# Query and key projections by Strassen's scheme, gate steps with one operand in PSUM, and a new order

## The chip, the cores and the metric

One core of a Trainium2 chip runs one program. The metric is the device time of one execution in microseconds, as the median of several runs. The engines are named as in the profile: PE is TensorE's matmul, PEld its weight load, DVE is VectorE, ACT is ScalarE, POOL is GpSimd, SP is SyncE, whose queue issues every transfer here.

## The reference

Two sequences of 768 tokens with 512 features pass through three layers, all in 32-bit floats.

```python
# 1 retention, 8 heads of 64, per token t
state = gamma * state + outer(k[t], v[t]);  x[t] = q[t] @ state / 8
# 2 channel MLP (2048 wide)
x = x + relu(norm(x) * g @ w1) @ w2
# 3 mixture of 4 attention experts (width 64), no residual
logits = x @ w_gate                     # the two best experts of each token, softmax over them
for e in range(4):
    q, k, v = x @ wq[e], x @ wk[e], x @ wv[e]
    a = softmax(causal(q @ k.T / 8))
    out += gate[:, e] * (a @ v @ wo[e])
```

## The kernel before

Tokens are handled in six chunks of 128 per sequence `b` and, in the wide layers, in two blocks `j` of 384 (`TB`). Each operand of a wide product is kept as a rounded high half and a rest (`h`, `l`; `x` holds `XH` and `XL`), and a product is three matmuls: high by high, high by rest, rest by high.

The stages are these.

- **Retention**, `r_tile`: for each of the twelve tiles (b, chunk) scores, `intra`, `inter`, a state update and two transposes on PE, with masks, norm and splitting on DVE, ACT and POOL. Its inputs `kq` and `vk` and the first weight pieces `raw` come in over SP.
- **Channel MLP**: eight slices `f` of 256 hidden features. For f = 0 and 1 `m_h` makes the hidden block and `m_c` multiplies it by the second weights and adds to the running sum `xT`. For f = 2 to 7 (`SEVEN`) the hidden block of a sequence is made by `m_h7`, which uses Strassen's scheme: seven products (six matmuls each) where eight would be needed, over a two by two split of weights (by `S`, made in `w_sums` on POOL) and of tokens and features (by `t`, made once per sequence in `x_sums` on POOL and ACT). The partial results are combined with `keep` (ACT copies PSUM to `u`) and `add` (DVE). The last slice ends with new `XH`, `XL` for the third layer.
- **Projections**: `q_proj` makes queries and keys of one block (two halves of the contraction, six matmuls each), `q_val` makes values and logits of a chunk, `gates` turns the logits of a block into weights with twelve small DVE instructions and one on ACT.
- **Attention**: `a_scores` (PE, DVE, ACT, DVE, POOL in turn), `a_turn` (transposes), `a_value`, `a_out`, sequence 0 first, with the work of sequence 1 between.

All instructions are steps of a planner, `Plan`. A step names an engine, a cost, what it reads and writes and its buffers; its priority is its place in the program plus a bias plus a number of the table `RANK`, and `issue` lets each engine take the ready step with the lowest priority whose buffers have room. What comes out is a fixed order on each engine, and buffers at fixed places (`PL`). The same table decides when each transfer is issued. PSUM has eight banks, `ps`. At the start PE fills time with matmuls on a constant tile (`spin`).

## Time and profile before

| | |
|---|---|
| median of 3 runs | 439.39 us (438.41 to 439.47) |
| the profiled execution's own time | 436.77 us |
| its span in the trace | 435.0 us |
| PE busy | 426.4 us, 98% of the span |
| PEld, DVE, ACT, POOL busy | 401.7, 300.6, 216.3, 213.5 us |
| clock granted to PE | full in every slice |

The profiled execution took 1.8 us more than the span of its trace, and 2.6 us less than the median of the runs. A busy PE counts matmuls of any tile, the constant ones of the start too.

### The profile page before, as it was taken

The numbers are of one execution on the slowest core, as the hardware profiler recorded it, in microseconds if no ns is written. First come the engines' busy times: TensorE is split into PE (matmuls) and PEld (weight loads), VectorE is DVE, ScalarE is ACT, GpSimd is POOL, SyncE is SP. The second block draws the span as 40 slices with busy tenths as digits, with TensorE's granted clock in tenths as the row PEclk, the third lists the DMA queues.
The fourth block names the chain that finished last, engine by engine and source line by source line (L and its number), as shares of the span: only waits on it lengthen the run. The fifth ranks groups of instructions, "written<-read, shape, count | busy, mean of one in ns | idle before, by whom it ended". The sixth has DMA issues, their size and how long they took to land.

```text
span 435.0 us, 9093 instructions
## 1 busy us (share of the span) xinstructions
PE 426.4 (98%) x3546; PEld 401.7 (92%) x3546; DVE 300.6 (69%) x756; ACT 216.3 (50%) x458; POOL 213.5 (49%) x224
## 2 busy tenths in 40 slices
PE   8998999999999999999999999999999999999996
PEld 7777998999999999999999999999999899877875
DVE  2769999855558876966966764458936776778762
ACT  1568676242557436436336234324621775778540
POOL 1777877999999616416316126400130533251530
PEclk9999999999999999999999999999999999999999
DMA  7999723200232202303304001102000000010212
GB/s 270 327 343 319 232 83 111 105 2 0 87 108 98 98 2 96 99 0 100 95 2 132 15 1 35 63 2 75 23 6 2 2 2 0 3 50 26 75 60 88
DMA packets 11995, 35.18 MB, mean 81 GB/s; under 512 B 1840, under 2 KB 2480, under 8 KB 11952
## 3 DMA queue, kind: packets, MB, share of 16 engines
q1 hardware_dynamic: 11952, 34.60, 23.2%
q8 instruction: 28, 0.46, 0.4%
q14 instruction: 15, 0.12, 0.1%
HBM read 31.45 MB, written 3.15 MB: 80 GB/s over the span
## 4 chain that ended last, share of the span: by engine, by line
PE 91%; DVE 2%; DMA 1%; issue 0%; POOL 0%; ACT 0%; SPq 0%; POOLq 0%
PE ps L791 31%; PE ps L861 20%; PE ps L769 8%; PE ps L955 8%; PE ps L1124 4%; PE ps L979 4%; PE ps L425 4%; PE ps L1050 4%; PE ps L1151 4%; PE ps L613 1%; DMA vk<-in_vk_dram 1%; PE ps L584 1%; PE ps L621 1%; PE ps L603 0%; DVE xT L633 0%; DVE ps L695 0%
## 5 line engine op out<-in xcount | busy, mean ns | idle before, releaser
L791 PE MATMUL ps<-h,w 128*128 128x384 f32 x768 | 144.3, 335 | 0.0
L791 PEld LDWEIGHTS ps<-h,w 128*128 128x128 f32 x768 | 133.8, 188 | 0.7 <-issue 0.2
L797 DVE TENSOR_TENSOR xT<-xT,ps 128x384 f32<-128x384 f32 x112 | 60.6, 551 | 32.6 <-PE ps L791 31.9
L1080 POOL TENSOR_SCALAR pr<-pr,sm,gate 128x384 f32<-128x384 f32 (+5 forms) x48 | 33.9, 718 | 66.4 <-ACT pr L1065 26.0
L722 POOL TENSOR_TENSOR w<-wy,w 128x512 fp32r<-128x512 f32 x26 | 33.4, 1296 | 42.1 <-PE ps L791 39.7
L861 PE MATMUL ps<-t,S 128*128 128x384 f32 x216 | 42.2, 335 | 0.0
L861 PEld LDWEIGHTS ps<-t,S 128*128 128x128 f32 x216 | 37.7, 188 | 0.3 <-DVE wy L698 0.3
L769 PE MATMUL ps<-x,w 128*128 128x384 f32 x192 | 35.4, 337 | 0.0
L688 ACT ACTIVATE wx<-raw 128x512 f32<-128x512 f32 x32 | 21.7, 678 | 26.2 <-DVE ps L695 15.4
L1065 ACT ACTIVATE pr<-pr,sm 128x384 f32<-128x384 f32 (+5 forms) x48 | 31.7, 662 | 5.2 <-DVE sm L1057 5.1
L769 PEld LDWEIGHTS ps<-x,w 128*128 128x128 f32 x192 | 33.2, 188 | 0.5 <-DVE xT L797 0.2
L870 ACT ACTIVATE u<-ps 128x384 f32<-128x384 f32 x36 | 17.4, 489 | 31.5 <-PE ps L861 24.9
L880 ACT ACTIVATE h<-ps 128x384 fp32r<-128x384 f32 x48 | 23.1, 488 | 18.6 <-PE ps L791 13.2
L875 DVE TENSOR_TENSOR ps<-ps,u 128x384 f32<-128x384 f32 x36 | 20.3, 563 | 16.4 <-ACT u L870 10.3
L690 POOL TENSOR_SCALAR wx<-wx 128x512 f32<-128x512 f32 x32 | 19.8, 618 | 23.2 <-ACT wx L688 22.7
L861 PE MATMUL ps<-x,w 128*128 128x384 f32 x144 | 28.5, 334 | 0.0
L882 DVE SCALAR_TENSOR_TENSOR h<-ps,h 128x384 fp32r<-128x384 f32 x48 | 26.0, 551 | 2.8 <-ACT h L880 2.7
L692 DVE TENSOR_SCALAR ps<-wx 128x512 uint32<-128x512 uint32 x32 | 22.0, 688 | 4.9 <-POOL wx L690 4.9
L861 PEld LDWEIGHTS ps<-x,w 128*128 128x128 f32 x144 | 25.3, 188 | 0.0
L720 ACT ACTIVATE w<-wy 128x512 fp32r<-128x512 f32 x26 | 16.3, 628 | 17.2 <-PE ps L791 17.0
L698 DVE SCALAR_TENSOR_TENSOR wy<-raw,ps 128x512 uint32<-128x512 uint32 x32 | 21.9, 684 | 3.8 <-POOL sf L738 2.1
L1057 DVE CUSTOM_DVE_ANT_0 pr<-ps,mask 128x384 f32<-128x384 f32 (+4 forms) x48 | 22.0, 495 | 2.3 <-PE ps L1050 2.1
(116 smaller groups left out, 797.7 us busy)
## 6 DMA issues: line engine op xcount, KB each, us to landing
raw<-in_w_dram SPq DMA_DIRECT2D x32, 512.0 KB, 3.5
kq<-in_kq_dram SPq DMA_DIRECT2D x11, 512.0 KB, 5.5
vk<-in_vk_dram SPq DMA_DIRECT2D x9, 512.0 KB, 5.6
out_dram<-ob SPq DMA_DIRECT2D x11, 256.0 KB, 2.0
vk<-in_vk_dram SPq DMA_DIRECT2D x4, 256.0 KB, 5.3
vraw<-in_wv_dram SPq DMA_DIRECT2D x1, 520.0 KB, 3.4
kq<-in_kq_dram SPq DMA_DIRECT2D x2, 256.0 KB, 2.9
mraw<-in_wk_dram SPq DMA_DIRECT2D x1, 512.0 KB, 3.6
```

Of the source, the lines that this page charges most:

```text
L692: DVE(0.69, lambda: dve.tensor_scalar(u32(z), u32(x), 4, 1, op0=OP.logical_shift_left, op1=OP.logical_shift_right), r=[x], w=[z])
L722: POOL(1.3, lambda: pool.tensor_tensor(f32r(l), f32(y), f32(h), OP.subtract), r=[y, h], w=[l])
L769: pe.matmul(f32(pa, TB), lhsT=wt, rhs=blk(f32r(xt[b][j]))[:, k], start=(n == 0), stop=(n == 11))
L791: pe.matmul(f32(pa, TB), lhsT=wt, rhs=t, start=(n == 0), stop=(n == 5))
L797: DVE(0.55, lambda: dve.tensor_tensor(blk(f32(xt))[:, k], blk(f32(xt))[:, k], f32(pa, TB), OP.add), r=[pa] + [(xt, cc, w) for cc in range( ...
L861: pe.matmul(f32(pa, TB), lhsT=wt, rhs=t, start=(first and n == 0), stop=(n == 5), skip_group_check=True)
L880: ACT(0.49, lambda: act.activation(f32r(h, TB), f32(src, TB), AF.Relu), r=[src], w=[h])
L882: DVE(0.55, lambda: dve.scalar_tensor_tensor(f32r(l, TB), f32(src, TB), 0.0, f32(h, TB), op0=OP.max, op1=OP.subtract), r=[src, h], w=[l])
L955: pe.matmul(f32(pa, TB), lhsT=mw(n, lo, k, p * 128, (p + 1) * 128), rhs=blk(f32r(xt))[:, k], start=(i == 0), stop=(i == 11))
L1057: DVE(0.22 + wide * 1.04e-3, lambda ks=ks, n=n, z=z, SC=SC: dve.tensor_tensor_reduce(f32(PR[z])[:, ks], f32(SC[z])[:, :wide], f32(MASK)[:, ...
L1065: ACT(act_c(nk) + .18, lambda pr=pr, z=z: act.activation(f32(pr, nk), f32(pr, nk), AF.Exp, bias=f32(sm)[:, z:z + 1], scale=-1.0, accum_out ...
L1080: POOL(0.34 + nk * 0.84e-3, lambda pr=pr, z=z, e=e: pool.tensor_scalar(f32(pr, nk), f32(pr, nk), f32(sm)[:, 6 + z:7 + z], GT[b, j][:, cc, ...
```

## The change

- `q_proj` is now one call for a sequence and a weight: seven products of six matmuls over a two by two split, where four blocks of twelve matmuls stood. It brings `keep` and `add` steps, and buffers `uq`.
- The split weights `Sq` of `wk` and `wq` are made in `load_mw` on POOL (four small operations, one large) and ACT.
- The split tokens `t` have to be made anew from the third layer's input: `x_sums(b, False)` runs for both sequences at the end of the channel MLP, four subtractions and four rests on POOL and four copies on ACT each. For that the last `m_c` also writes its result to `xT` on ACT.
- In `gates` one operand of each two-operand step lies in PSUM, behind one more copy; each of its two DVE steps takes a PSUM bank.
- In `q_phase` the values and gates come ahead of queries and keys, queries and keys of the two sequences change places in memory, and `pr` has eleven buffers where it had twelve.
- All numbers of `RANK` are new, so the order on every engine is.

```diff
-    "q_proj 1": (32, (137, -8, -29, -4, 36, 0, 0, -70)),
...
-    "x_sums 2": (8, (-50, -134, 8, -63, 8, 11, -28, -102)),
...
+    "q_proj 1": (28, (8, -5, -10, -14, 50, -3, 112, 73)),
...
+    "x_sums 2": (16, (1, 0, -66, 56, -9, 0, -18, 20)),
...
+    PL["Sq"] = region(o_z, 4 * KB, 2) + region(o_h + 28 * KB, 4 * KB, 2)
+    PL["uq"] = region(o_z + 8 * KB, 3 * KB // 2, 4)
...
-    PL["qk0"] = region(o_r, 3 * KB, 8)
-    PL["vv0"] = region(o_r + 36 * KB, KB, 6)
+    PL["qk0"] = region(o_h, 3 * KB, 8)
+    PL["vv0"] = region(o_h + 36 * KB, KB, 6)
...
-    PL["qk1"] = region(o_h, 3 * KB, 8)
-    PL["vv1"] = region(o_h + 36 * KB, KB, 6)
-    PL["pr"] = region(o_xt, 3 * KB, 8) + region(o_h + 24 * KB, 3 * KB, 4)
+    PL["qk1"] = region(o_r, 3 * KB, 8)
+    PL["vv1"] = region(o_xt + 18 * KB, KB, 6)
+    PL["pr"] = region(o_xt, 3 * KB, 6) + region(o_r + 36 * KB, 3 * KB, 4) + region(o_h + 24 * KB, 3 * KB, 1)
...
         ACT(0.49, lambda: act.activation(blk(f32r(xh))[:, k], f32(pa, TB), AF.Copy),
...
         P.at = "m_c 5"
+        ACT(0.49, lambda: act.activation(blk(f32(xt))[:, k], f32(pa, TB), AF.Copy), r=[pa], w=[(xt, "k", k)])
+        P.at = "m_c 6"
         DVE(0.55, lambda: dve.tensor_tensor(blk(f32r(xl))[:, k], f32(pa, TB), blk(f32(xh))[:, k], OP.subtract),
-            r=[pa, (xh, "k", k)], w=[(xl, "k", k)] + (keys(xl) if k == 0 else []))
+            r=[pa, (xt, "k", k), (xh, "k", k)], w=[(xl, "k", k)] + (keys(xl) if k == 0 else []))
 
...
-    def x_sums(b):
+    def x_sums(b, own=True):
         th, tl = TH[b], TL[b]
         both = lambda fn, r, w: POOL(1.85, lambda: fn(pool), r, w)
-        for t, kh, j in ((2, 0, 1), (0, 0, 0), (1, 1, 1), (3, 1, 0)):
+        for t, kh, j in ((2, 0, 1), (0, 0, 0), (1, 1, 1), (3, 1, 0)) if own else ():
             cs = slice(kh * TW, (kh + 1) * TW)
             P.at = "x_sums 1"
             both(lambda en, t=t, j=j, cs=cs: en.tensor_tensor(plain(tl[t]), f32(XH[b][j])[:, cs], f32(XL[b][j])[:, cs], OP.add),
                  keys(XH[b][j]) + keys(XL[b][j]), [tl[t]])
-        for t, p, q in ((0, 2, 0), (2, 1, 2), (1, 1, 0), (3, 3, 1)):
+        xs = {2: (0, 1), 0: (0, 0), 1: (1, 1), 3: (1, 0)}
+
+        def part(t, new):
+            if own or new:
+                return lambda: plain(tl[t]), [tl[t]]
+            kh, j = xs[t]
+            return lambda: f32(XT[b][j])[:, kh * TW:(kh + 1) * TW], [(XT[b][j], "k", 2 * kh + k) for k in range(2)]
+
+        for t, p, q, made in ((0, 2, 0, ()), (2, 1, 2, ()), (1, 1, 0, (0,)), (3, 3, 1, (1,))):
+            (xp, rp), (xq, rq) = part(p, p in made), part(q, q in made)
             P.at = "x_sums 2"
-            both(lambda en, t=t, p=p, q=q: en.tensor_tensor(plain(tl[t]), plain(tl[p]), plain(tl[q]), OP.subtract),
-                 [tl[p], tl[q]], [tl[t]])
+            both(lambda en, t=t, xp=xp, xq=xq: en.tensor_tensor(plain(tl[t]), xp(), xq(), OP.subtract), rp + rq, [tl[t]])
         for t in range(4):
             P.at = "x_sums 3"
             ACT(0.84, lambda t=t: act.activation(f32r(th[t]), plain(tl[t]), AF.Copy), r=[tl[t]], w=[th[t]])
...
         P.at = "load_mw 3"
         POOL(2.4, lambda: pool.tensor_tensor(f32r(l, sz), f32(raw, sz), f32(h, sz), OP.subtract), r=[raw, h], w=[l])
...
+        if n in ("wk", "wq"):
+            sh, sl = new("Sq"), new("Sq")
+            at = lambda i, m: f32(raw)[:, 512 * i:512 * i + 512].rearrange("p (k m c) -> p k m c", k=2, m=2)[:, :, m]
+            part = lambda i: plain(sl)[:, 256 * i:256 * i + 256].rearrange("p (k c) -> p k c", k=2)
+            for i, p, q, op in ((0, lambda: at(0, 1), lambda: at(1, 1), OP.add),
+                                (1, lambda: part(0), lambda: at(0, 0), OP.subtract),
+                                (2, lambda: at(0, 0), lambda: at(0, 1), OP.subtract),
+                                (3, lambda: at(1, 0), lambda: part(1), OP.subtract)):
+                P.at = "load_mw 4"
+                POOL(0.76, lambda i=i, p=p, q=q, op=op: pool.tensor_tensor(part(i), p(), q(), op), r=[raw], w=[sl])
+            P.at = "load_mw 5"
+            ACT(1.1, lambda: act.activation(f32r(sh), plain(sl), AF.Copy), r=[sl], w=[sh])
+            P.at = "load_mw 6"
+            POOL(2.41, lambda: pool.tensor_tensor(f32r(sl), plain(sl), f32(sh), OP.subtract), r=[sl, sh], w=[sl])
+            MW[n, "S"] = (sh, sl)
...
-    def q_proj(b, j, n, p):
-        cs = slice(j * TB, (j + 1) * TB)
-        pa = new("ps")
-        xh, xl = XH[b][j], XL[b][j]
-        for hf in range(2):
-            def mm(hf=hf):
-                i = 6 * hf
-                for k in (2 * hf, 2 * hf + 1):
-                    for lo, xt in ((0, xh), (0, xl), (1, xh)):
-                        pe.matmul(f32(pa, TB), lhsT=mw(n, lo, k, p * 128, (p + 1) * 128), rhs=blk(f32r(xt))[:, k],
-                                  start=(i == 0), stop=(i == 11))
+    def q_proj(b, n):
+        sh, sl = MW[n, "S"]
+
+        def product(pa, wn, xn, first):
+            h, l = (sh, sl) if wn[0] == "s" else MW[n][:2]
+            c0, step = (256 * int(wn[1]), 128) if wn[0] == "s" else ((512 if wn[0] == "y" else 0) + 128 * int(wn[1]), 256)
+            if xn[0] == "t":
+                xs = TH[b][int(xn[1])], TL[b][int(xn[1])]
+                xr, xat = list(xs), lambda k: tuple(f32r(t)[:, k * TB:(k + 1) * TB] for t in xs)
+            else:
+                kh, xs = int(xn[1]), (XH[b][int(xn[2])], XL[b][int(xn[2])])
+                xr, xat = xkeys(xs[0]) + xkeys(xs[1]), lambda k: tuple(blk(f32r(t))[:, 2 * kh + k] for t in xs)
+
+            def mm():
+                i = 0
+                for k in range(2):
+                    wh, wl = (f32r(t)[:, c0 + k * step:c0 + k * step + 128] for t in (h, l))
+                    xh, xl = xat(k)
+                    for wt, t in ((wh, xh), (wh, xl), (wl, xh)):
+                        pe.matmul(f32(pa, TB), lhsT=wt, rhs=t, start=(first and i == 0), stop=(i == 5), skip_group_check=True)
                         i += 1
             P.at = "q_proj 1"
-            PE(1.06, mm, r=list(MW[n][:2]) + xkeys(xh) + xkeys(xl) + ["seven"], w=[pa])
-        hi, lo = (QK[n, y, b, p] for y in range(2))
-        by = 0.125 if n == "wq" else 1.0
-        P.at = "q_proj 2"
-        ACT(0.485, lambda: act.activation(f32r(hi)[:, cs], f32(pa, TB), AF.Copy, scale=by), r=[pa], w=[(hi, j)])
-        P.at = "q_proj 3"
-        DVE(0.556, lambda: dve.scalar_tensor_tensor(f32r(lo)[:, cs], f32(pa, TB), by, f32(hi)[:, cs], op0=OP.mult, op1=OP.subtract),
-            r=[pa, (hi, j)], w=[(lo, j)])
+            PE(1.04, mm, r=[h, l] + xr + ["seven"], w=[pa])
+
+        def keep(pa):
+            u = new("uq")
+            P.at = "q_proj 2"
+            ACT(0.49, lambda: act.activation(f32(u), f32(pa, TB), AF.Copy), r=[pa], w=[u])
+            return u
+
+        def add(dst, pa, u):
+            P.at = "q_proj 3"
+            DVE(0.55, lambda: dve.tensor_tensor(f32(dst, TB), f32(pa, TB), f32(u), OP.add), r=[pa, u], w=[dst])
+
+        def out(src, p, j):
+            cs = slice(j * TB, (j + 1) * TB)
+            hi, lo = (QK[n, y, b, p] for y in range(2))
+            by = 0.125 if n == "wq" else 1.0
+            P.at = "q_proj 4"
+            ACT(0.485, lambda: act.activation(f32r(hi)[:, cs], f32(src, TB), AF.Copy, scale=by), r=[src], w=[(hi, j)])
+            P.at = "q_proj 5"
+            DVE(0.556, lambda: dve.scalar_tensor_tensor(f32r(lo)[:, cs], f32(src, TB), by, f32(hi)[:, cs], op0=OP.mult, op1=OP.subtract),
+                r=[src, (hi, j)], w=[(lo, j)])
+
+        pa, pb, pc = (new("ps") for _ in range(3))
+        product(pa, "a0", "x00", True)
+        c1 = keep(pa)
+        product(pb, "s1", "t1", True)
+        add(pb, pb, c1)
+        product(pa, "y0", "x10", False)
+        out(pa, 0, 0)
+        u2 = keep(pb)
+        product(pc, "s0", "t0", True)
+        product(pb, "s2", "t2", False)
+        u3 = keep(pb)
+        c22 = new("ps")
+        add(c22, pc, u3)
+        product(pb, "y1", "t3", False)
+        out(pb, 1, 0)
+        product(pc, "s3", "x11", False)
+        add(pc, pc, u2)
+        out(pc, 0, 1)
+        out(c22, 1, 1)
...
-        g = LG[b, j]
+        g, z1, z2 = LG[b, j], new("ps"), new("ps")
         G = GT[b, j]
         sh = [128, TPB, E, E]
-        lg = lambda: f32(g)[:, 0:12].rearrange("p (t e) -> p t e", e=E)
-        gt = lambda: f32(g)[:, 16:64].rearrange("p (t e f) -> p t e f", e=E, f=E)
-        eq = lambda: f32(g)[:, 64:112].rearrange("p (t e f) -> p t e f", e=E, f=E)
-        w = lambda: f32(g)[:, 112:124].rearrange("p (t e) -> p t e", e=E)
-        mx = lambda: f32(g)[:, 124:127]
+        three = lambda ap: ap.rearrange("p (t e) -> p t e", e=E)
+        four = lambda ap: ap.rearrange("p (t e f) -> p t e f", e=E, f=E)
+        lg = lambda: three(f32(g)[:, 0:12])
+        gt = lambda: four(f32(g)[:, 16:64])
+        w = lambda: three(f32(g)[:, 112:124])
 
         def one():
-            lf = lg()[:, :, None, :].to_broadcast(sh)
+            zl, zm = three(f32(z1)[:, 0:12]), f32(z1)[:, 124:127]
+            ze = four(f32(z1)[:, 64:112])
+            lf = zl[:, :, None, :].to_broadcast(sh)
             le = lg()[:, :, :, None].to_broadcast(sh)
+            dve.tensor_copy(zl, lg())
             dve.tensor_tensor(gt(), lf, le, OP.is_gt)
-            dve.tensor_tensor(eq(), lf, le, OP.is_equal)
-            dve.tensor_tensor(eq(), eq(), before[:, None].to_broadcast(sh), OP.mult)
-            dve.tensor_tensor(gt(), gt(), eq(), OP.add)
-            dve.tensor_reduce(mx(), lg(), axis=AX, op=OP.max)
-            dve.tensor_tensor(w(), lg(), mx()[:, :, None].to_broadcast([128, TPB, E]), OP.subtract)
+            dve.tensor_tensor(ze, lf, le, OP.is_equal)
+            dve.tensor_tensor(ze, ze, before[:, None].to_broadcast(sh), OP.mult)
+            dve.tensor_tensor(gt(), ze, gt(), OP.add)
+            dve.tensor_reduce(zm, zl, axis=AX, op=OP.max)
+            dve.tensor_tensor(w(), lg(), zm[:, :, None].to_broadcast([128, TPB, E]), OP.subtract)
         P.at = "gates 1"
-        DVE(1.1, one, r=[(g, cc) for cc in range(TPB)] + ["before"], w=[(g, "one")])
+        DVE(1.5, one, r=[(g, cc) for cc in range(TPB)] + ["before"], w=[(g, "one"), z1])
...
         def two():
-            rk = f32(g)[:, 64:76].rearrange("p (t e) -> p t e", e=E)
-            sm = f32(g)[:, 80:83]
+            rk, sm = three(f32(z2)[:, 0:12]), f32(z2)[:, 16:19]
...
-        DVE(1.25, two, r=[(g, "one"), (g, "w")], w=[("G", b, j)])
+        DVE(1.5, two, r=[(g, "one"), (g, "w")], w=[("G", b, j), z2])
...
     DMA(64e3, lambda: sp.dma_start(f32(MASK)[:, S - C:], a["future"]), r=list(MW["wv"][:2]), w=[(MASK, 1)])
+    x_sums(0, False)
     flush()
+    x_sums(1, False)
 
     def q_phase(b):
         q_alloc(b)
         for j in range(NB):
-            for n in ("wk", "wq"):
-                for p in range(2):
-                    q_proj(b, j, n, p)
-            P.bias += 20 * (b + 1)
             for t in range(TPB):
                 q_val(b, TPB * j + t)
             gates(b, j)
-            P.bias -= 20 * (b + 1)
+        for n in ("wk", "wq"):
+            q_proj(b, n)
```

The order changes everywhere; three places matter below.

The first is SP's queue at its start, the transfers in the order of issue (`kq` and `vk` are a tile's inputs, `caus`, `tabV` and `tab` constants; numbers tell buffers apart). Before:

```order
L498 DMA kq_82<-in_kq_dram 128x512 x2
L503 DMA caus<-in_caus_dram 128x128
L501 DMA tabV<-in_tabV_dram 128x48
L508 DMA vk_90<-in_vk_dram 128x512
L516 DMA tab_3_94<-in_tabY_dram 128x512
L508 DMA vk_90<-in_vk_dram 128x512
```

and now:

```order
L510 DMA tabV<-in_tabV_dram 128x48
L507 DMA kq_83<-in_kq_dram 128x1024
L507 DMA kq_88<-in_kq_dram 128x512 x2
L517 DMA vk_94<-in_vk_dram 128x512
L512 DMA caus<-in_caus_dram 128x128
L517 DMA vk_94<-in_vk_dram 128x512
```

`kq_88` and `vk_94` belong to the first tile; `kq_83` is that of the third tile (sequence 0, chunk 1), whole, and now stands ahead of them. Further down the two first weight pieces `raw` are issued as numbers 17 and 18 of the queue, where they were 26 and 27, ahead of five `vk` and four `kq` that they used to follow.

The second is POOL where the channel MLP ends. Before, it had four rests of weights left to make and the mask:

```order
L928 TENSOR_TENSOR wk_3220<-mraw_3180,wk_3212 128x1024
L928 TENSOR_TENSOR wq_3241<-mraw_3189,wq_3224 128x1024
L928 TENSOR_TENSOR wo_3559<-mraw_3515,wo_3548 128x1024
L928 TENSOR_TENSOR wv_3584<-vraw_3496,wv_3537 128x1040
L1226 MEMSET mask_3604 128x640
```

Now it comes from the split weights and makes the split tokens of sequence 0, then those of sequence 1 (L844 are the subtractions, L849 the rests):

```order
L962 TENSOR_TENSOR Sq_3460<-Sq_3332,Sq_3449 128x1024
L844 TENSOR_TENSOR t_1334<-xT_636,xT_154 128x768
L844 TENSOR_TENSOR t_1312<-xT_636 128x768
L844 TENSOR_TENSOR t_1352<-xT_636,t_1334 128x768
L844 TENSOR_TENSOR t_1375<-xT_154,t_1352 128x768
L849 TENSOR_TENSOR t_1441<-t_1334,t_1411 128x768
L849 TENSOR_TENSOR t_1476<-t_1352,t_1444 128x768
L849 TENSOR_TENSOR t_1494<-t_1312,t_1446 128x768
L947 TENSOR_TENSOR wo_3621<-mraw_3521,wo_3607 128x1024
L849 TENSOR_TENSOR t_1510<-t_1375,t_1478 128x768
L947 TENSOR_TENSOR wv_3658<-vraw_3541,wv_3619 128x1040
L844 TENSOR_TENSOR t_1535<-xT_703,xT_238 128x768
```

On PE the last eight `m_c` are those of sequence 1; behind them stand eleven products of sequences 0 and 1, then the first `q_val`. The first two read `x` and need no `t`; the third needs `t_1441`, the fourth `t_1476`, the tenth `t_1510`, and `q_val` needs `wv_3658`.

The third is PE in the attention of sequence 0, where the work of sequence 1 stands between (L1050 and L1128 are scores, L425 and L434 transposes, L955 and L999 projections). Before, where a projection ends:

```order
L955 MATMUL ps<-x_1062,wq_3224 128x384
L955 MATMUL ps<-x_1034,wq_3241 128x384
L1050 MATMUL ps<-qk_490_3582,qk_493_3594 128x384 x2
L1050 MATMUL ps<-qk_490_3582,qk_494_3596 128x384 x2
L1050 MATMUL ps<-qk_492_3586,qk_493_3594 128x384 x2
L425 MATMUL ps<-ident,pr_3854 128x64 x2
L425 MATMUL ps<-ident,pr_3879 128x64 x2
```

and now:

```order
L999 MATMUL ps<-x_407,wk_3197 128x384
L1128 MATMUL ps<-qk_503_3678,qk_518_3832 128x512 x2
L1128 MATMUL ps<-qk_503_3678,qk_520_3859 128x512 x2
L1128 MATMUL ps<-qk_505_3682,qk_518_3832 128x512 x2
L434 MATMUL ps<-ident,pr_3934 128x64 x2
L434 MATMUL ps<-ident,pr_3959 128x64 x4
L999 MATMUL ps<-t_1787,Sq_3246 128x384
```

What was a stretch of 72 matmuls of `q_proj` in a row and a few shorter ones is now taken one product at a time. From the first projection to the end PE's order has 21 stretches of matmuls on full 128 by 128 weights where it had 14, and 50 changes of tile shape where it had 34; before that point it has 9 stretches where it had 13, and 56 changes where it had 60.

## Rows read from the trace of the kernel before

**Rows 1.** The page: span, busy time, data rate by slice, chain that ended last.

```profile
span 435.0 us, 9093 instructions
PE 426.4 (98%) x3546; PEld 401.7 (92%) x3546; DVE 300.6 (69%) x756; ACT 216.3 (50%) x458; POOL 213.5 (49%) x224
...
GB/s 270 327 343 319 232 83 111 105 2 0 87 108 98 98 2 96 99 0 100 95 2 132 15 1 35 63 2 75 23 6 2 2 2 0 3 50 26 75 60 88
...
PE 91%; DVE 2%; DMA 1%; issue 0%; POOL 0%; ACT 0%; SPq 0%; POOLq 0%
```

**Rows 2.** Windows: length, busy by engine, granted clock, DMA share, GB/s.

```profile
0.00:45.00 45.00, 40.03 (x694) 34.70 (x696) 28.93 (x68) 24.84 (x52) 26.18 (x37) 1.00 0.90 313
...
100.00:312.00 212.00, 212.00 (x1222) 211.39 (x1221) 146.64 (x272) 95.63 (x185) 100.39 (x90) 1.00 0.18 58
312.00:372.00 60.00, 59.86 (x488) 57.71 (x486) 36.09 (x146) 29.17 (x68) 18.52 (x19) 1.00 0.01 2
372.00:432.00 60.00, 59.50 (x672) 46.51 (x670) 43.17 (x177) 36.80 (x101) 20.83 (x32) 1.00 0.13 48
```

**Rows 3.** The chain in order of time: start, us, what, matmuls.

```profile
45.24 4.39 PE ps L769 x24
...
106.19 4.16 PE ps L791 x24
...
312.59 11.44 PE ps L955 x66
324.03 1.43 PE ps L979 x12
...
348.73 1.24 PE ps L955 x6
...
359.50 12.71 PE ps L955 x72
...
373.80 1.63 PE ps L979 x12
```

**Rows 4.** Timeline of PE, first 50 us: start, us, instructions, idle time before.

```profile
1.05 4.30 PE L532 MATMUL ps<-negs 128*128 128x128 f32 x20 [1.05 <-DVE half L549]
...
6.38 0.94 PE L532 MATMUL ps<-negs 128*128 128x128 f32 x6
...
8.05 1.09 PE L613 MATMUL ps<-am,vs 128*64 128x128 f32 x16 [0.74 <-POOL vs L574]
...
45.17 4.46 PE L769 MATMUL ps<-x,w 128*128 128x384 f32 x24
```

**Rows 5.** Groups by line and form: busy us, mean ns, idle time before.

```profile
L870 ACT ACTIVATE u<-ps 128x384 f32<-128x384 f32 x36 | 17.4, 489 | 31.5 <-PE ps L861 24.9 <-DVE ps L875 6.1 <-DVE h L882 0.5
...
L875 DVE TENSOR_TENSOR ps<-ps,u 128x384 f32<-128x384 f32 x36 | 20.3, 563 | 16.4 <-ACT u L870 10.3 <-PE ps L861 6.1
```

**Rows 6.** Groups by line and form, POOL alone.

```profile
L830 POOL TENSOR_TENSOR t<-t,t 128x768 fp32r<-128x768 f32 x8 | 14.8, 1861 | 0.2
L824 POOL TENSOR_TENSOR t<-t,t 128x768 f32<-128x768 f32 x8 | 14.8, 1852 | 0.1
...
L738 POOL TENSOR_TENSOR sf<-wy,wy 128x256 f32<-128x256 f32 x6 | 4.5, 745 | 2.4 <-ACT wy L704 2.4
...
L928 POOL TENSOR_TENSOR wv<-vraw,wv 128x1040 fp32r<-128x1040 f32 x1 | 2.4, 2437 | 0.1
...
L928 POOL TENSOR_TENSOR wo<-mraw,wo 128x1024 fp32r<-128x1024 f32 x1 | 2.4, 2402 | 34.3 <-ACT wo L926 34.3
```

**Rows 7.** Timelines of ACT and DVE at the end of the channel MLP.

```profile
313.15 0.87 ACT L804 ACTIVATE x<-ps 128x384 fp32r<-128x384 f32 x2
...
312.82 0.56 DVE L801 TENSOR_TENSOR ps<-ps,xT 128x384 f32<-128x384 f32 x1
```

**Rows 8.** The tile ga (the gates), durations in ns: min/median/max.

```profile
L991 DVE COPY ga<-ps x12: 144/152/164, 325.8 to 399.0; 128x4 f32<-128x4 f32 x12
...
L1027 DVE TENSOR_SCALAR ga<-ga x4: 169/169/641, 333.5 to 401.4; 128x3 f32<-128x3 f32 x4
```

More of the change, by code (lines that the diff above doesn't have):

```diff
@@ L60 @@
 QUEUES = {"ps1": "s", "ps2": "s", "pr": "pr", "pt": "pt", "ptn": "pt", "sm": "sm", "at": "at", "w": "w", "h": "h", "raw": "raw", "wy": "wy",
-          "w1": "w1", "S": "S", "t": "t", "u": "u", "sf": "sf",
+          "w1": "w1", "S": "S", "t": "t", "u": "u", "Sq": "Sq", "uq": "uq", "sf": "sf",
           "am": "am", "vs": "vs", "xn": "xn", "xc": "xc"}
-ROUNDED = {"x", "w", "w1", "S", "t", "h", "wq", "wk", "wv", "wo", "qk0", "qk1", "at"}
+ROUNDED = {"x", "w", "w1", "S", "Sq", "t", "h", "wq", "wk", "wv", "wo", "qk0", "qk1", "at"}
 class Buf:
```

153 rows, old and new, of the table RANK are left out of this document.

## The prediction

> **What bounds the kernel now.** I read the page first. PE is busy for 426.4 of 435.0 us and makes up 91% of the chain that ended last [rows 1]; no other engine passes 70%. The windows then say where the other 8.6 us lie: in the first 45 us PE is busy for 40.03, from 100 to 312 us for all 212.00, from 312 to 372 us for 59.86 and from there to 432 us for 59.50 [rows 2]. So from 45 us on the kernel lasts as long as PE has matmuls, and a matmul less is time less. Only the start is different: constant matmuls (4.30 us before the first scores, 0.94 us behind them), then a wait of 0.74 us for POOL's first product, and the first block of the MLP only at 45.17 us [rows 4], while transfers run at 327 to 343 GB/s in the second to fourth slice [rows 1]. There PE is paced by data. Behind the last matmul stand a copy and a transfer, which the change leaves as they are.
>
> **The products.** 66 matmuls of `q_proj` in a row take 11.44 us [rows 3], 1.04 us for six. Before there are 2 sequences x 2 weights x 2 blocks x 2 halves of columns x 12 matmuls = 192, or 32 sixes, 33.28 us. Now there are 2 x 2 x 7 = 28 sixes, 29.12 us. On PE this is **-4.16 us**, and as PE has no idle time there it counts in full.
>
> **Changes of shape.** The chain shows what a stretch of matmuls on full 128 by 128 weights costs when matmuls of other tile shapes stand on both sides. `q_val` (x12) takes 1.63 us there and 1.43 us among its like; six matmuls of `q_proj` 1.24 instead of 1.04; 72 of them 12.71 instead of 12 x 1.04 = 12.48; 24 of `m_h` 4.39, where 24 in the MLP take 4.16 [rows 3]. That is 0.20 to 0.23 us a stretch. From the projections on PE's order has 21 such stretches for 14: 7 x 0.21 = +1.5 us. Before them it has 9 for 13: 4 x 0.22 = -0.9 us. Together **+0.6 us**. The bounds are 0 (the added stretches fall where PE would wait anyway) and +1.5 (the ones saved at the start only lengthen a wait for data). The Trainium skill, "TensorEngine Tiling (Array Packing)", Key Properties, speaks against this part of the change: switching the tiling mode drains the engine, whichever mode follows. By that rule all changes of shape count, 50 for 34 and 56 for 60, 12 more net, and at half a stretch's 0.21 us each the term would be +1.3 instead of +0.6.
>
> **The new work on POOL, ACT and DVE.** POOL gets two sets of `Sq` at 4 x 0.745 + about 2.4 us and two sets of `t` at 4 x 1.85 + 4 x 1.86 [rows 6]: 10.8 + 29.7 = 40.5 us. ACT gets some 22 us: 16 + 12 copies at 0.49, as of their kind [rows 5], eight of 768 columns, two of 1024. DVE gets 12 adds at 0.56 [rows 5] and four copies of 0.15 in `gates` [rows 8]. None of it is on PE, and POOL is idle for half of the span [rows 1], so it costs nothing where it is ready in time. `Sq` is: it follows the MLP's last sums on POOL, and before there was nothing to do for POOL there until the rests of `wo` and `wv`. `t` is the question, as its input is the MLP's very last result. I count from the moment at which PE ends the last `m_c` of sequence 0.
>
> - PE has eight `m_c` of sequence 1 (8.32), two products without `t` (10.40 us), then wants `t_1441`; the fourth product wants `t_1476` at 11.44, the tenth `t_1510` at 17.68, `q_val` wants `wv_3658` at 19.76.
> - POOL can begin the second subtraction once DVE has added (0.56) and ACT has written `x` and `xT` (0.49 each): at about 1.6. Three subtractions of 1.85 and a rest of 1.86 give `t_1441` at 9.0, the next rest `t_1476` at 10.9, a third and `wo` (2.40) and a fourth `t_1510` at 17.0, and `wv` (2.44) is there at 19.4 [rows 6]. The margins are 1.4, 0.5, 0.7 and 0.3 us.
> - ACT must have kept the first product in `uq` before the seventh product adds to the same bank, at 8.32 + 6 x 1.04 = 14.56. Ahead of that keep stand the last copies of sequence 1, which can't end before PE's last `m_c` and DVE's add, some 9.5; behind it come about three copies, `wo`, two copies and `wv`, at 0.38 between the starts of two copies [rows 7] and about 1.0 for a large one: 13.4, and the keep ends at 13.9. The margin is 0.7.
>
> Every margin is positive and none is wide. Before, DVE starts its last add of the MLP at 312.82 us [rows 7], when PE had gone on to the projections at 312.59 [rows 3] already, so the helpers do run some 0.5 us behind. I take **+0.4 us** for a wait here, 0 below, and 1.5 above (0.8 us more of lag than margin on POOL, and the same again on ACT). What waits behind is everything on PE.
>
> **The gates** cost nothing: they are 12 instructions of 0.15 to 0.2 us and now 13, on a DVE that is busy for 36.09 of 60 us there [rows 2], and only POOL's step in `a_scores` waits for them. Without that cover it would be 4 x 0.15 = 0.6 us. Two banks less for a moment cost nothing while a bank is free; their price, if not, is in the attention's waits.
>
> **The attention.** Its chain from scores over DVE, ACT, DVE, POOL back to a transpose needs other work on PE between. There are 28 - 14 = 14 products of sequence 1 left for that, 2.1 us less than before, and spread more evenly. 0.50 us of 60 are idle there now [rows 2]. I take **+0.3 us**, from 0 to 1.5.
>
> **The start.** Work on PE is the same. The input of the third tile now goes first, 0.52 MB at some 335 GB/s, 1.6 us; and the first two `raw`, 1.05 MB or 3.1 us, go ahead of five `vk` and four `kq`. The first delays the first scores (three more constant matmuls of 0.43 us fill the time, 4.30 / 10, a matmul being two records [rows 4]) and spares a transfer later; the second delays tiles and lets `m_h` fill PE earlier. The queue's total up to the tenth tile's scores, counted from its order and the tensors' sizes, is about equal (12.0 MB against 12.2). I take **0**, from -2 (PE's waits among the tiles shrink, of some 5 us idle) to +4.4 (all of 3.1 and 1.3 us shows).
>
> **Sum.** -4.16 + 0.6 + 0.4 + 0.3 = -2.9 us. The profiled execution would go from 436.77 to 433.9 us; it lies 2.6 us under the median of the runs, so the median would go from 439.39 to **436.5 us**.
>
> **Rivals.** What a measurement of this kernel can tell from no change is about 0.3%, 1.3 us: faster is under 438.1, slower over 440.7.
>
> - *The forecast*, 435.2 to 437.9: 0.52.
> - *The start gains too*: with the first weights, 17th and 18th in SP's queue instead of 26th and 27th, on chip some 10 us earlier, the first `m_h` comes forward and the tiles' waits are filled with it. For it: 5 us idle (45.00 less 40.03) [rows 2] and over 5 us of constant matmuls [rows 4] to win from. Against: it also needs the first block of `x`, whose tiles' inputs come no earlier. -2 more gives 434.5: 0.17.
> - *`t` comes late*: ACT and POOL have most of the new work within 20 us, and if the last copies of sequence 0 wait on ACT behind others, all of POOL's chain shifts. It eats the gain when `t_1441` comes 4 us later than reckoned, less the margin of 1.4: +2.6 gives 439.1. For it: POOL's row is strict, `wo` and `wv` stand within it. Against: the margins. 0.13.
> - *Every change of shape costs a whole stretch's 0.21 us*: 16 more at the end are +3.4, and the start gives nothing back. -4.16 + 3.4 + 0.7 gives 439.3. For it: transposes between scores now alternate with products. Against: 0.20 to 0.23 covers both ends of a stretch. This is, at its dearest, what the Trainium skill says in "TensorEngine Tiling (Array Packing)", Key Properties. 0.08.
> - *Slower*: the start is paced by transfers, and 3.1 + 1.3 us of them have been put ahead of what the first tiles need. If PE reaches the first `m_h` only at 49.6 us instead of 45.17 [rows 4], 436.5 becomes 440.9. The point from which it decides is 4.2 us of delay there. For it: the transfer engines are busy for 0.90 of the first 45 us [rows 2]. Against: `m_h` itself can then start at once and fill. 0.10.
>
> Faster is 0.52 + 0.17 and a little of the third, 0.70; same 0.19; slower 0.11. For 8 in 10 the range must take in the better start and the late `t`: 433.7 to 439.8.
>
> **What will show it.** Right: `q_proj` at 28 x 1.04 us on PE; no wait of PE on POOL's or ACT's rows between the MLP and the first `q_val` beyond a microsecond; PE's first `m_h` between 43 and 47 us; PE busy from there on. Wrong: PE idle ahead of the third, fourth, seventh or tenth product (then the chain names `t` or `uq`); stretches of `q_proj` in the attention at clearly more than 1.25 us; a first `m_h` past 49 us.

## The result and the profile after

| | before | after |
|---|---|---|
| median, first comparison | 438.9 us (4 runs) | 434.16 us (4 runs, 433.82 to 435.13) |
| ratio, 95% interval | | 0.9899 (0.9871 to 0.9928) |
| median, second comparison | 438.23 us (11 runs) | 434.46 us (6 runs) |
| ratio, 95% interval | | 0.9915 (0.9898 to 0.9932) |
| first profiled execution: time, span | 436.77, 435.0 us | 435.13, 433.3 us |
| second profiled execution: time, span | 438.09, 436.2 us | 434.51, 432.7 us |

The change gains 3.8 to 4.7 us, about 1%, where 2.9 were forecast. The first profiled execution of before was a quick one (436.77, other runs up to 439.78), and the first of the change a slow one. So I took both kernels a second time, and compare the executions near the medians, 438.09 and 434.51. Two executions far from all others, one of 520.14 us at a mean granted clock of 0.754 and one of 1438.83 us, are left out of the medians below.

The page of the changed kernel, its span and busy times (these answer to [rows 1]):

```profile
span 433.3 us, 9152 instructions
PE 425.2 (98%) x3522; PEld 397.8 (92%) x3522; DVE 306.3 (71%) x770; ACT 233.6 (54%) x494; POOL 253.8 (59%) x251
```

The windows of [rows 2]; columns as there:

```profile
100.00:312.00 212.00, 212.00 (x1219) 210.72 (x1219) 144.74 (x267) 101.94 (x200) 120.81 (x106) 1.00 0.18 58
312.00:372.00 60.00, 60.00 (x481) 55.07 (x482) 45.27 (x178) 39.16 (x91) 36.52 (x29) 1.00 0.01 2
```

The chain in order of time, from the first projection on ([rows 3]):

```profile
312.50 11.44 PE ps L999 x66
...
347.92 1.25 PE ps L999 x6
...
354.38 4.37 PE ps L999 x24
```

PE is the bound as before. Sixty-six matmuls in a row still take 11.44 us, and a product of six alone in the attention takes 1.25 where four products in a row take 4.37, 1.09 each. POOL is busy for 36.52 us of the window from 312 to 372, twice what it was, and PE for all 60.00. Two times split the kernel well: the start of PE's first product of the projections, and the end of the span. From PE's timelines, that product in the second profile of before and of after:

```profile
313.74 1.20 PE L955 MATMUL ps<-x,wk 128*128 128x384 f32 x6
```

```profile
311.77 1.20 PE L999 MATMUL ps<-x,wk 128*128 128x384 f32 x6
```

| | first product at | from there to the end of the span |
|---|---|---|
| before, first and second profile | 312.43, 313.74 | 122.57, 122.46 |
| after, first and second profile | 312.34, 311.77 | 120.96, 120.93 |

Behind that point the change gains 1.5 to 1.6 us, the same in each pair. Ahead of it, it gains 0.1 us by the first profiles and 1.97 by the second. The medians of 438.23 and 434.46 us lie 3.8 apart, which leaves about 2.2 us ahead of it in a usual execution. Nearly all that lies between two executions of a kernel lies in the start, too: 1.31 of 1.32 us in before, 0.57 of 0.62 in the change.

### The profile page after: what moved, and what is told of

Read it like the earlier page. It is cut to its first block, busy times and chain, and to the rows that moved or that the text cites. A ratio compares the mean times of both kernels' runs of the same rounds, so it can differ in the third digit from the quotient of the medians.

```text
span 433.3 us, 9152 instructions
## 1 busy us (share of the span) xinstructions
PE 425.2 (98%) x3522; PEld 397.8 (92%) x3522; DVE 306.3 (71%) x770; ACT 233.6 (54%) x494; POOL 253.8 (59%) x251
## 4 chain that ended last, share of the span: by engine, by line
PE 90%; DMA 4%; POOL 2%; DVE 1%; issue 1%; ACT 1%; SPq 1%; DVEq 0%; POOLq 0%; ACTq 0%
PE ps L800 31%; PE ps L880 20%; PE ps L999 7%; PE ps L778 6%; PE ps L1202 5%; PE ps L1229 4%; PE ps L1128 4%; PE ps L434 4%; PE ps L1055 4%; DMA vk<-in_vk_dram 3%; PE ps L593 1%; PE ps L622 1%; DMA decay<-in_decay_dram 1%; PE ps L612 1%; POOL vs L583 1%
## 5 line engine op out<-in xcount | busy, mean ns | idle before, releaser
L800 PE MATMUL ps<-h,w 128*128 128x384 f32 x768 | 140.5, 335 | 0.0
L849 POOL TENSOR_TENSOR t<-t,t 128x768 fp32r<-128x768 f32 x16 | 29.3, 1856 | 0.3
```

The lines of the kernel that those rows point to most:

```text
L800: pe.matmul(f32(pa, TB), lhsT=wt, rhs=t, start=(n == 0), stop=(n == 5))
L849: both(lambda en, t=t: en.tensor_tensor(f32r(tl[t]), plain(tl[t]), f32(th[t]), OP.subtract), [tl[t], th[t]], [tl[t]])
```

## The experiments

### The kernel before, once more

> The kernel before once more, for a second profile and more runs. The profiled execution of before took 436.77 us, its other runs 437.71 to 439.47. Theory A (the part of the gain that was not forecast lies in the start: before usually loses 1 to 3 us more there than in the execution that was profiled): a profiled execution of 438 us or more shows PE's eighth m_h or first m_c 1 to 3 us later than 59.89 us, and from there on the same. Theory B (it lies behind the start, in waits of the attention): the same start, and the longer time between 312 us and the end. Ratio 1.000.

438.0 us (437.05 to 439.78), ratio 0.9998 (0.9981 to 1.0015). The first `m_c` of the profiled execution starts at 61.27 us, 1.4 later than the 59.89 of the first one, and from there on it takes as long. Up to 100 us PE does the same 928 matmuls of start and retention in every kernel here, so what it has done beyond them by then are MLP matmuls of 0.173 us. Windows of the first 100 us, this kernel and then the change's second profile:

```profile
0.00:100.00 100.00, 94.13 (x1162) 84.91 (x1163) 73.82 (x161) 54.77 (x105) 72.42 (x84) 1.00 0.56 195
```

```profile
0.00:100.00 100.00, 95.83 (x1177) 87.58 (x1178) 74.46 (x164) 53.86 (x102) 73.51 (x85) 1.00 0.55 195
```

The number behind PE's time counts: 1162 against 1177, 15 more, or 2.6 us. (The first profiles have 1170 and 1173.) From 100 to 312 us the change gives back half a microsecond: x1222 in [rows 2], x1219 in its own row above. Theory A holds for the start. How the time up to the projections is made up stands in the section on the prediction.

### The two starts exchanged

Each step's number in the table comes from the other kernel for loads, retention tiles, the first eight weight pieces and `m_h`:

```diff
 def rank(at):
-    n, r = RANK.get(at[0], (1, (0,)))
+    table = RANK
+    if at[0]:
+        name = at[0].split(" ")[0]
+        if name in FIRST_OF and at[1] < UP_TO.get(at[0], UP_TO.get(name, 99)):
+            table = FIRST
+    n, r = table.get(at[0], (1, (0,)))
```

The changed kernel with the start of before:

> The changed kernel with the order of before in its start (loads, tiles, first eight weight pieces, first MLP block), and its own order from the projections on. Theory A: the start's part of the gain is lost, 436 to 437.3 us. Theory B: 434.2, as the change as a whole.

> The changed kernel with the order of before in its start once more, for a profile at full clock. It was 439.87 us, slower than both kernels. Theory A': the start loses about 2 us against the change, and the rest is a wait in the MLP or behind it that the mixed order makes, of 2 to 3 us, with a stretch at half clock behind it. Theory B': nothing is lost in the start, and all 5.7 us lie in such a wait.

439.71 us, ratio to before 1.0035 (1.002 to 1.0051), and 440.45 in one more run, from which the profile is. By 100 us PE has done 1159 matmuls, 18 fewer than the change: 3.1 us. Its first product comes at 317.67 us, and from there to the end it takes 121.03 us, as the change does. That is 5.9 us later than in the change. The rest of the loss lies in the MLP, with two waits there of 0.65 and 0.58 us; some 1.6 us of it I did not follow. Theory A' is right in kind, but the granted clock stays at 1.00, so there is no stretch at half clock.

The kernel before with the start of the change:

> The kernel before with the changed kernel's order in its start alone. Theory A: 436 to 437 us, 2 to 3 us faster than before. Theory B: 438.9, as before. The forecast's own term for the start was 0, from -2 to +4.4.

442.45 us, ratio 1.009 (1.0064 to 1.0117): the wrong sign for both theories. Its first 100 us are the best of all in busy time (96.32 us, 1173 matmuls), but then the mixed order makes PE wait in the MLP. The timeline of PE, and the windows there (columns as above; the number ahead of the DMA share is the granted clock):

```profile
148.86 1.86 PE L908 MATMUL ps<-t,S 128*128 128x384 f32 x6 [2.00 <-ACT u L917]
151.29 2.29 PE L908 MATMUL ps<-t,w 128*128 128x384 f32 x6 [0.58 <-ACT u L917]
```

```profile
145.00:150.00 5.00, 3.00 (x16) 2.68 (x15) 3.80 (x6) 2.11 (x3) 3.66 (x4) 0.94 0.22 61
150.00:152.00 2.00, 1.42 (x5) 0.91 (x4) 1.40 (x3) 1.25 (x3) 0.12 (x1) 0.50 0.43 129
...
156.00:158.00 2.00, 2.00 (x12) 2.00 (x11) 1.58 (x4) 0.87 (x2) 2.00 (x2) 0.95 0.00 0
```

The waits add up to 2.6 us. Behind the first of them the clock falls to 0.50, the lower of its two levels, 1.2 GHz, and stays there until 156 us; the second wait already lies in that stretch. The total tells nothing of the start, the first 100 us do: both exchanged kernels come within 3 matmuls of a count of the start that they were given (1159 for 1162 or 1170, 1173 for 1173 or 1177), and pay elsewhere for an order that was made for another start.

### The first two weight pieces late

```diff
 def rank(at):
+    if at[0] == "load_piece 1" and at[1] < 2:
+        return 200
     n, r = RANK.get(at[0], (1, (0,)))
```

> The changed kernel with its first two weight pieces put back to places 27 and 28 of the transfer queue, where before had them (26 and 27); from the middle of the MLP on the order is the same. Theory A'' (the start gains because the pieces land earlier and DVE splits them in time that it spent idle): DVE's first split begins near 36 us instead of 24, PE's lost time up to 100 us goes from about 12.7 to 14.5 to 15 us, and the time is 436 to 436.5 us. Rival (the gain is in the order of the tiles): no split before 30 us either, but 12.7 us lost and 434.2 us.

443.21 us, ratio to before 1.0139 (1.0109 to 1.0169), more than theory A'' had said. Windows of the first 100 us:

```profile
0.00:100.00 100.00, 91.43 (x1140) 81.77 (x1141) 72.48 (x159) 52.59 (x99) 68.79 (x82) 1.00 0.55 195
```

1140 matmuls instead of 1177: 6.4 us lost. In the first 30 us PE is better off, busy for 28.37 us (25.88 and 26.33 in the change's two profiles), from 30 to 60 us it has 23.92 (29.79 and 29.50). PE's idle time by what it waited for shows DVE at the top, 5.6 us in all up to 100 us:

```profile
PE ps L614 <- DVE am L601: 2.6, 2, 1.7
PE ps L780 <- DVE xT L644: 1.8, 1, 1.8
```

DVE's timeline shows why. First, the second profile of before, then the change (the first operation of a piece's split has line 692 in one and 701 in the other, and the bracket is idle time ahead of an operation):

```profile
25.94 1.29 DVE L590 TENSOR_TENSOR am<-ps,caus 128x512 f32<-128x512 f32 x2 [1.00 <-PE ps L584]
...
37.88 0.69 DVE L692 TENSOR_SCALAR ps<-wx 128x512 uint32<-128x512 uint32 x1
```

```profile
24.26 0.68 DVE L701 TENSOR_SCALAR ps<-wx 128x512 uint32<-128x512 uint32 x1
```

Before, DVE sits idle eight times between 15 and 35 us, 6.5 us in all, mostly for want of PE's results, and its first split begins at 37.88. In the change it begins at 24.26, in that idle time; from 40 to 50 us, where DVE had been busy for 9.1 of 10 us, it has 7.3 now. PE's waits for DVE among the tiles are 1.9 us in each profile of before and 0.4 in each of the change; those for POOL rise, in the second profiles from 1.8 to 2.5, and those for ACT and transfers fall there from 0.7 to nothing. With the pieces late the split begins at 38.74 again, and POOL is waited for 0.2 us.

So the changed order needs its pieces early, and DVE is where their lateness shows. This run loses more than the two orders differ by, so it doesn't say that the early pieces are the whole gain, and the third tile's input, which now goes first, was not moved by itself.

### The gates back in SBUF

```diff
         def one():
-            zl, zm = three(f32(z1)[:, 0:12]), f32(z1)[:, 124:127]
-            ze = four(f32(z1)[:, 64:112])
+            zl, zm = lg(), f32(g)[:, 124:127]
+            ze = four(f32(g)[:, 64:112])
...
-            dve.tensor_copy(zl, lg())
...
-            rk, sm = three(f32(z2)[:, 0:12]), f32(z2)[:, 16:19]
+            rk, sm = three(f32(g)[:, 64:76]), f32(g)[:, 80:83]
```

> The changed kernel with the gates' operands back in SBUF and without the four extra copies; the order on every engine is otherwise the same. The forecast says the gates are hidden behind other work of DVE: 434.2, no difference. Rival: with both operands in SBUF the DVE steps wait for POOL's operations on t at the same time (one of them took 641 ns in the trace of before, where 169 is usual), and the time grows by up to 1 us.

441.89 us (441.48 to 442.34), ratio to before 1.0084 (1.0058 to 1.0111): 7.4 us slower than the change, with the same order on every engine. The forecast's reason falls, and the rival was right in kind and far too small in size. Timelines of DVE, POOL and PE, and the windows behind:

```profile
328.44 1.88 DVE L1089 TENSOR_TENSOR ga<-ga 128x48 f32<-128x48 f32 x1
330.35 1.76 DVE L1090 TENSOR_TENSOR ga<-ga,before 128x48 f32<-128x48 f32 x1
332.15 1.73 DVE L1091 TENSOR_TENSOR ga<-ga 128x48 f32<-128x48 f32 x1
...
333.99 1.73 DVE L1093 TENSOR_TENSOR ga<-ga 128x12 f32<-128x12 f32 x1
```

```profile
328.41 3.64 POOL L849 TENSOR_TENSOR t<-t,t 128x768 fp32r<-128x768 f32 x2
332.01 1.80 POOL L844 TENSOR_TENSOR t<-xT,t 128x768 f32<-128x768 f32 x1
333.89 1.80 POOL L849 TENSOR_TENSOR t<-t,t 128x768 fp32r<-128x768 f32 x1
```

```profile
337.12 2.97 PE L1055 MATMUL ps<-wv,x 128*128 128x260 f32 x12 [4.50 <-DVE ga L1067]
...
343.03 4.46 PE L1055 MATMUL ps<-wv,x 128*128 128x260 f32 x36
```

```profile
341.00:342.00 1.00, 1.00 (x5) 1.00 (x4) 0.90 (x6) 0.00 (x0) 0.16 (x1) 0.50 0.00 0
...
343.00:344.00 1.00, 1.00 (x11) 1.00 (x10) 0.79 (x6) 0.00 (x0) 0.00 (x0) 1.00 0.00 0
```

The same four steps in the change, and POOL beside them:

```profile
329.14 0.21 DVE L1090 TENSOR_TENSOR ps<-ps,ga 128x48 f32<-128x48 f32 x1
329.38 0.22 DVE L1091 TENSOR_TENSOR ps<-ps,before 128x48 f32<-128x48 f32 x1
329.63 0.21 DVE L1092 TENSOR_TENSOR ga<-ps,ga 128x48 f32<-128x48 f32 x1
...
330.08 0.17 DVE L1094 TENSOR_TENSOR ga<-ga,ps 128x12 f32<-128x12 f32 x1
```

```profile
329.02 3.66 POOL L849 TENSOR_TENSOR t<-t,t 128x768 fp32r<-128x768 f32 x2
```

Four small operations take 1.73 to 1.88 us, where the change takes 0.21 or 0.22 for each of 48 elements and 0.17 for the one of 12. Each has two inputs in SBUF, and each ends with one of POOL's operations on `t`: the first of them starts at 328.44 beside POOL's pair of 328.41 to 332.05. In the change the steps stand beside the same pair of POOL's, with one input in PSUM. The Trainium skill, "SBUF — State Buffer", Who interferes with whom, says that a DVE instruction with two SBUF inputs contends with a GpSimd instruction that reads SBUF, as its second input comes through the pair of ports that they share, and that the loser is blocked for the whole instruction. The rows agree. The row of 641 ns that the expectation names is another case: that step has one input, and it ended at 362.97 us, with an operation of POOL's in the attention that ended at 362.95.

Behind the gates DVE's copies are late that free PE's banks (L1067 takes the logits out of one), PE stands still for 4.50 us, and its clock is at 0.50 until 342 us. From the wait's end, 337.12, to 343.03 PE does what the change does in 3.54 us (333.06 to 336.60): 2.4 us. 4.5 and 2.4 are 6.9 of the 7.0 us by which this execution is longer behind the first product (127.96 against 120.93).

### The split tokens late

```diff
-            both(lambda en, ...: en.tensor_tensor(plain(tl[t]), xp(), xq(), OP.subtract), rp + rq, [tl[t]])
+            def sub(en, t=t, xp=xp, xq=xq, again=2 if not own and b == 0 and t == 2 else 0):
+                for _ in range(1 + again):
+                    en.tensor_tensor(plain(tl[t]), xp(), xq(), OP.subtract)
+            both(sub, rp + rq, [tl[t]])
```

In the change itself the timelines of POOL and of PE give the margins:

```profile
311.05 5.46 POOL L849 TENSOR_TENSOR t<-t,t 128x768 fp32r<-128x768 f32 x3
...
318.84 1.84 POOL L849 TENSOR_TENSOR t<-t,t 128x768 fp32r<-128x768 f32 x1
320.63 2.45 POOL L947 TENSOR_TENSOR wv<-vraw,wv 128x1040 fp32r<-128x1040 f32 x1
```

```profile
314.42 4.32 PE L999 MATMUL ps<-t,Sq 128*128 128x384 f32 x24
...
321.70 1.20 PE L999 MATMUL ps<-t,wk 128*128 128x384 f32 x6
...
323.78 7.33 PE L1055 MATMUL ps<-wv,x 128*128 128x260 f32 x60
```

The three rests end at 312.9, 314.7 and 316.5, and PE wants the first at 314.42 and the second one product later, at 315.46: margins of 1.5 and 0.75 us. The fourth ends at 320.68 for 321.70, and `wv` at 323.08 for 323.78, margins of 1.0 and 0.7. The forecast had 1.4, 0.5, 0.7 and 0.3.

> The changed kernel with one subtraction of the split tokens of sequence 0 done three times on POOL, 2 x 1.86 = 3.7 us more ahead of the first t; order otherwise the same. In the trace of the change POOL has the t for PE's third product 1.55 us early and that for the fourth 0.75 us early. If those are the margins, PE waits for 3.7 - 0.75 = 3.0 us in all and the time is 437.2 us; with a clock that falls to half behind a wait of 2 us, as it did in the run with the gates in SBUF, another 2 to 3 us: 439 to 440. Rival (the wait is absorbed, since PE later has other slack): under 435.5.

439.22 us, ratio to before 1.0025 (1.0006 to 1.0045). The size is what the halved clock would make of it: seven of nine runs have a mean granted clock of 0.992 to 0.996 and take 438.8 to 440.9 us, the other two 0.998 and 1.000 and take about 437.7. (The wait of 2 us that the expectation names is that of the exchanged starts, 2.00; in the run with the gates PE waited 4.50.) But the wait stands elsewhere. Timelines of PE, ACT and DVE, and a window of one microsecond behind the wait:

```profile
313.94 3.02 PE L800 MATMUL ps<-h,w 128*128 128x384 f32 x12 [3.04 <-DVE x L818]
```

```profile
311.69 0.84 ACT L850 ACTIVATE t<-t 128x768 fp32r<-128x768 f32 x1 [3.53 <-POOL t L846]
```

```profile
313.33 0.56 DVE L818 TENSOR_TENSOR x<-ps,x 128x384 fp32r<-128x384 f32 x1 [3.90 <-ACT xT L816]
```

```profile
316.00:317.00 1.00, 1.00 (x5) 1.00 (x4) 0.00 (x0) 1.00 (x4) 1.00 (x1) 0.50 0.00 0
```

It is an `m_c` of sequence 1 that waits, ahead of all projections. ACT's queue has a copy of `t` (L850) ahead of copies of the last `m_c`; it waits for POOL for 3.53 us, DVE behind it for 3.90, and the `ps` banks that they would free are what PE wants. Of 3.72 us of delay 3.04 arrive at PE: the narrowest margin on this way is 0.7 us, and it is not one of those that I had counted.

### The plain projections in the new order

`q_proj` is that of before, with its three rows of the table; `Sq` and the copy to `xT` are left out, and gates, other numbers and buffers are those of the change.

```diff
-    x_sums(0, False)
     flush()
-    x_sums(1, False)
...
         for n in ("wk", "wq"):
-            q_proj(b, n)
+            for j in range(NB):
+                for p in range(2):
+                    q_proj(b, j, n, p)
```

> The changed kernel with the plain projections of before (192 matmuls), without split tokens, split weights and the copies made for them; start, MLP and gates are those of the changed kernel, PE's first 2024 instructions the same. Theory A (the start gains about 2 us, the Strassen part about 1.6 us net of shape changes): 435.7 to 436.3 us, 2 us faster than before and 1.6 to 2 us slower than the change, and the projections begin at 311 to 312.4 us. Theory B (the start gains nothing): 438 us as before. Rival (the products count in full, 4.16 us): 438.3 us.

447.4 us, ratio 1.0211 (1.019 to 1.0233). The first product comes at 312.03 us, as theory A had it, but from there to the end it takes 133.7 us. A window near the end:

```profile
400.00:432.00 32.00, 29.44 (x298) 21.16 (x296) 26.18 (x97) 20.95 (x52) 14.86 (x20) 0.89 0.17 64
```

PE is idle for 2.6 of 32 us and the mean clock is 0.89. Behind the first product PE waits for 3.75 us in all, where the change waits for 0.3. That the attention's order was made for other work is the likely reason, but nothing here shows it. Neither theory is met, and this run doesn't give the price of the Strassen part.

### Changes of tile shape by themselves

```diff
             n = 0
+            for h in range(2 if 2 <= f <= 6 else 0):
+                hs = slice(0, 64)
+                pe.matmul(f32(pa)[hs, 32 * h:32 * h + 32], lhsT=ident[hs, hs], rhs=ident[hs, 0:32], start=True, stop=True)
             for m in range(2):
```

> The changed kernel with two small constant matmuls (32 columns, 32-bit floats, weights 128 by 128) ahead of each of the 80 m_c products of f = 2 to 6, overwritten by the product: no change of tile shape. By the constant matmuls of the start (0.43 us for 128 columns) 80 x 2 x 0.11 = 17 us more, about 451 us. The control for the next two.

> The same with weights 64 by 64 (one quarter of the array): each pair now ends a stretch of full-weight matmuls and begins another. If a stretch costs 0.21 us, as the forecast took it, 80 x 0.21 = 16.8 us above the control, less what a quarter of the weights loads faster. If changes of shape cost nothing by themselves: the control's time.

> The same pairs, but the first with weights 64 by 64 and the second 64 by 128: one more change of shape in each excursion, 80 in all, and the same number of stretches. If only the full-weight stretches count (the forecast): as the 64 by 64 pairs. If every change counts alike (the rule that it set beside that): 80 x 0.1 = 8 us above them.

469.52, 477.82 and 496.02 us, one run each. PE's timelines, in this order (each small matmul is two records, so a pair is x4):

```profile
154.78 0.53 PE L797 MATMUL ps<-ident 128*128 128x32 f32 x4
155.15 1.29 PE L802 MATMUL ps<-h,w 128*128 128x384 f32 x6
156.27 2.24 PE L882 MATMUL ps<-t,S 128*128 128x384 f32 x12
```

```profile
154.05 0.41 PE L798 MATMUL ps<-ident 64*64 64x32 f32 x4
154.40 1.32 PE L803 MATMUL ps<-h,w 128*128 128x384 f32 x6
155.64 0.41 PE L798 MATMUL ps<-ident 64*64 64x32 f32 x4
```

```profile
156.87 0.63 PE L798 MATMUL ps<-ident 64*64 64x32 f32 x4
157.43 1.31 PE L804 MATMUL ps<-h,w 128*128 128x384 f32 x6
158.68 0.63 PE L798 MATMUL ps<-ident 64*64 64x32 f32 x4
```

The control costs more than I had reckoned, 35 us or 0.44 a pair. Against it the pair of 64 by 64 costs 8.3 / 80 = 0.10 us more, half of the 0.21 that the forecast took for a stretch: the product behind it takes 1.24 to the next start where it took 1.12, and 1.15 where another product follows instead of a pair. One more change, from 64 by 64 to 64 by 128, costs 18.2 / 80 = 0.23 us, as much as a whole stretch in [rows 3], though the number of full-weight stretches is the same. So a count of full-weight stretches alone is not enough. This is the side of the Trainium skill's rule in "TensorEngine Tiling (Array Packing)", Key Properties: each change of mode drains the engine. But the price is not one number, and why the step between the two small shapes is the dearer one is open. A pair of two 64 by 128 was not run, so the shape itself may have a part in the 0.23.

### The changed kernel, once more

> The changed kernel once more, for more runs and a second profile. Three profiles with before's start lost 13.7 to 15.3 us of PE up to 100 us, five with the new start 12.6 to 13.2. If the gain is made of about 2 us there and 1.6 us from the projections on, the median is 434.2 us, 3.6 to 4.2 under before's, and in this profile the projections begin between 311.3 and 312.4 us and the rest takes 121.0 us. Rival (the first four runs were lucky by 1 us or more): 435.2 us or more, as the execution profiled first.

434.46 us (433.82 to 435.46), ratio 0.9915 (0.9898 to 0.9932); the first product at 311.77 and 120.93 us behind it. The first four runs were not lucky.

## Why the prediction was right, and where it was not

The direction and the range held, but the median of 434.2 to 434.5 us lies under the band of 435.2 to 437.9 that the forecast itself was given. The start is the term that was mis-sized most; the second profiles, 3.5 us apart in span, show the sum. The measured parts are read from PE's timelines, each group counted to the start of the next, idle time left out.

| term | forecast | measured | by |
|---|---|---|---|
| products | -4.16 | -4.16 | 28 sixes at 1.04 |
| shapes, from the projections on | +1.5 | +2.5 | start to start, below |
| shapes, before them | -0.9 | -0.1 | constant matmuls -0.27, MLP +0.18 |
| wait for `t` and `uq` | +0.4 | 0 | no wait of PE there |
| attention waits | +0.3 | +0.1 | idle time from there on, 0.15 to 0.29 |
| the start | 0 | -1.9 | idle time 5.87 to 4.17, tiles -0.2 |
| sum | -2.9 | -3.5 | |

The first profiles, 1.7 us apart, agree with this in all but the start, where they give nothing: idle time falls by 0.6 and the tiles take 0.6 more. The 2.2 us that the medians leave ahead of the projections side with the second.

The parts behind the projections (second profile of before, then of after):

```
                       us       stretches      us       stretches
q_proj              33.98       6             31.18     13
q_val               17.80       6             17.51      4
a_out               18.13       8             18.61     10
scores              17.48      13             18.24     18
values              19.24       7             19.44      8
transposes          12.20      17             12.21     22
```

- **Products.** Right. `q_proj` falls by 2.80: 4.16 less 7 more stretches at 0.19.
- **Changes of shape.** The seven stretches more on full weights are there, and `q_proj`, `q_val` and `a_out` pay 1.36, 0.29 less and 0.48 more for them, 1.55 in all where I had 1.5. What the step left out are scores and values, +0.96 more, of which the scores alone are 0.76 over five stretches. So behind the projections the count of full-weight stretches failed, not their price. By the rule that I had set beside it, every change at half a stretch, 16 more would be 1.7; 2.5 is measured. Ahead of the projections the count was right, 9 for 13, and the gain is not there: the constant matmuls and those of the MLP take 0.1 us less where I had 0.9. Two of the four stretches saved were constant matmuls. The two saved in the MLP are worth about 0.4, and 0.5 is lost to four slow matmuls between 113 and 116 us, whose cause is open.
- **Late `t` and `uq`.** The margins were right within 0.4 us (that of `uq` was 1.0 for 0.7) and the wait of 0.4 that I added to them was wrong: it is 0. The way over ACT's queue and the banks of the last `m_c` was missed. It has 0.7 us to spare, no less than the others, so it did no harm.
- **The attention.** The 0.50 us of idle time that I read from [rows 2] is not idle time between matmuls: PE's work ends inside that window, at 431.5 us.

```profile
428.42 3.08 PE L1151 MATMUL ps<-wo,at 128*128 128x256 f32 x18
```

- **The gates.** "Cost nothing" is the right number with the wrong reason. I priced the operands in PSUM as a cost that DVE's idle time hides. They are what keeps DVE clear of POOL's new work on `t`, which now runs beside the gates; without them it costs 7.4 us and the change would be slower than before. The row of 641 ns in [rows 8] was a sign that POOL can hold up a step of the gates, though that step has one input.
- **The start.** The step that failed is "I take 0". The early pieces do delay the first tiles: with them late PE does 2.0 to 2.5 us more in the first 30 us. But the step weighed transfers and left out DVE. The pieces' work on DVE moves from time in which the tiles wait for DVE into time in which DVE waits for the tiles; in the second profiles 1.7 us of PE's idle time go, and its waits for DVE shrink by 1.5, while the other waits nearly cancel. PE's first `m_h` comes at 43.4 and 42.8 us, where it came at 45.2 and 46.6. The rival "the start gains too" is right about the start, -2 us, and its reason, waits among the tiles that are filled, is half of it. That its 434.5 came true as well is in part luck: its sum was -4.9, and 3.8 is what the medians show.
- **The base.** The forecast was reckoned from 439.39 us, the median of three runs of before; eleven runs in the second comparison give 438.23. Of the 2.0 us by which 434.46 lies under 436.5, 1.2 come from this base and the rest from the larger gain. I also took the median to lie 2.6 us over the profiled execution for both kernels. The offset is spread in the start, and the change has less of it: 433.8 to 435.5, before 436.8 to 439.8.

## What to carry to other kernels

Where a change adds work to GpSimd, list what VectorE does beside it with two operands in SBUF, not only who waits for the new results. In a start paced by transfers ask which engine will be the last to finish its part of the loaded data, and give it the data while it is idle. Orders made by a planner belong together: half of one with half of another cost more than either, so a part's price is read by stretches of the trace, not from the total.
